# Attention of blocks two to six: four tiles' scores in one stretch of 32x64 tiles, one carried product for two heads

## The chip, the core and the metric

The kernel runs on one core of one Trainium2 chip. The metric is device time in microseconds (us) of one execution. Busy times and start times below come from one profiled execution of the kernel before. The engines are PE (TensorE, matmul), DVE (VectorE), ACT (ScalarE), POOL (GpSimd) and SP (SyncE, which only issues DMAs here); PEld is TensorE's weight load, which runs beside PE.

## What is computed

A gated linear attention over chunks of tokens feeds two feed-forward layers. Here batch is 4, H = 8 heads, S = 768 tokens, D = 32, N = 16; the kernel uses chunks of 64.

```python
for c in range(nc):                      # chunks, in order; a state [N, D] per head is carried
    L = np.exp(cum[:, :, :, None] - cum[:, :, None, :]) * causal
    M = np.einsum('bhin,bhjn->bhij', Cc, Bc) * L              # scores times decay
    y_intra = np.einsum('bhij,bhjd->bhid', M, xc)             # products
    y_inter = np.einsum('bhin,bhnd->bhid', Cc, state) * exp(cum)   # carried
    y[:, :, sl] = y_intra + y_inter
    state = decay_full * state + sum_j(Bc_j x_j decay_from_j)  # new state, then carry
x = y.transpose(0, 2, 1, 3).reshape(3072, 256)
h = x @ w_in;   x = np.maximum(0.01 * h, h) @ w_out           # first layer, 256 -> 2048 -> 256
h = x @ w_in2;  out = (h * np.cos(h)) @ w_out2                # second layer
```

## The kernel before

**Staging.** The tokens are cut into six blocks (b = 0 to 5 in the code, one to six here) of 4 batches x 128 tokens. A tile j is the 128 tokens of one batch in a block. Each block goes through attention, then a first-layer job, then a second-layer job; the jobs run in the order `JOBS = "000110101011"`. A job has 16 steps f, each a matmul group into `h` (lines 684 to 686: three products of high and low parts for each of two row halves) and one into `y` (lines 725 to 727). All are 128x512, in the first job and a half partly 128x256. Attention of block b+1 is put in between the steps of first-layer job b.

**Order.** All work is handed to a planner (class `Order`) with costs per engine, due times and slots of buffers. It fixes one order for each engine; on the chip each engine then takes its instructions in that order and waits on semaphores. PE order decides between which steps an attention stretch comes.

**Attention of a block.** For each tile: `scan` (line 466, DVE) makes the decays in `abc`; `bd` scales B in `tok`; `decay_c` (DVE or POOL) scales C in `head`. The two tiles of a pair then go through:

- `cb`, the scores (line 483): 8 matmuls of a tile, each with 64 rows of `head`, 64 weight columns and 128 columns of output, so that 64x64 pieces of the array work. `headp` has zeros where heads don't meet, and a row half r goes into columns 128r of a bank.
- `decay` (line 491, DVE): scores times decays, from PSUM into `abc`; one 128x512 operation for an even tile (in `att`, two banks), two of 128x256 for an odd one (in two `g` tiles of one bank).
- `products` (lines 504 and 508): 24 matmuls a tile, 64 rows by 32 weight columns by 64; lines 508 make the new state, 128x64 for each chunk s, where each 32 rows hold two heads.
- `carry` (line 542, DVE): old state times decay plus new state, read from PSUM.
- `carried` (line 517): 16 matmuls a tile, 32 rows by 32 columns by 64, each for one head and one chunk, so two heads share 32 state rows by having zeros in C.
- `x_hi` (line 529, ACT) and `x_lo` (line 533, DVE) take the pair's sum out of PSUM into `x1h` and `x1l`, the input of the next first-layer job.

In blocks two to six PE has five stretches of this: scores of pair one; products of pair one; carried of pair one together with scores of pair two; products of pair two; carried of pair two. Each matmul in fp32 stands as two passes in the trace (x16 for 8 matmuls).

## Time and profile before

| | us |
|---|---|
| median of 3 runs | 589.3 (589.26 to 589.36) |
| the profiled execution: span from first to last instruction | 586.7 |
| PE busy | 578.3 (99%) |
| PEld busy | 471.5 (80%) |
| ACT busy | 353.3 (60%) |
| DVE busy | 321.4 (55%) |
| POOL busy | 265.1 (45%) |

No device time is shown for the profiled execution itself, only its span; the median lies 2.6 us above that span. Busy PE is time with at least one matmul under way, ends modelled. The five attention stretches of blocks two to six lie at 53 to 75, 90 to 109, 141 to 160, 279 to 298 and 373 to 392 us.

### The profile page before, as it was taken

Reading aid. Unit: us, or ns where it says so; the run is one execution under the profiler, and the core shown is the slowest. Engines: PE = TensorE matmul, PEld = TensorE weight load, DVE = VectorE, ACT = ScalarE, POOL = GpSimd, SP = SyncE. Lnnn points to the kernel's source line nnn. Section 1 sums busy time; section 2 is a strip of 40 time slices with the busy share of each in tenths; the row PEclk is TensorE's granted clock in tenths of the full one; section 3 lists DMA queues with packets and bytes.
Section 4 is the critical chain, followed back from the end, with each engine's and each line's share of the span. In section 5 each row is a group of like instructions: output and inputs, shape, how many; then the busy total and the mean of one; then the engine's idle time right before and its main releaser. Section 6 shows DMA issues by size and latency. Waiting matters only on the chain.

```text
span 586.7 us, 11708 instructions
## 1 busy us (share of the span) xinstructions
PE 578.3 (99%) x4655; PEld 471.5 (80%) x4657; DVE 321.4 (55%) x610; ACT 353.3 (60%) x592; POOL 265.1 (45%) x224
## 2 busy tenths in 40 slices
PE   8899999999999999999999999999999999999996
PEld 4787887787788888888788888778888888888885
DVE  6999896845676656650464562121565002566664
ACT  4999767688856565554346554344755444655564
POOL 3221226188504455445525445443645444554442
PEclk9899999999999999999999999999999999999999
DMA  8994445543710001001330001000000100000101
GB/s 280 282 296 145 157 144 180 174 144 108 234 56 0 1 1 37 0 1 36 110 111 2 0 1 36 2 2 1 1 0 2 37 0 0 2 0 1 37 0 36
DMA packets 25798, 38.95 MB, mean 66 GB/s; under 512 B 2224, under 2 KB 8880, under 8 KB 25744
## 3 DMA queue, kind: packets, MB, share of 16 engines
q1 hardware_dynamic: 25744, 38.22, 20.6%
q8 instruction: 36, 0.59, 0.4%
q14 instruction: 18, 0.15, 0.1%
HBM read 34.96 MB, written 3.24 MB: 65 GB/s over the span
## 4 chain that ended last, share of the span: by engine, by line
PE 95%; DMA 2%; DVE 1%; SPq 0%; issue 0%; ACT 0%
PE y L725 15%; PE y L727 15%; PE y L726 15%; PE h L684 12%; PE h L685 11%; PE h L686 11%; PE g L686 4%; PE g L685 4%; PE g L684 4%; DMA tok<-tokp 1%; PE att L483 1%; PE att L517 1%; PE att L504 1%; PE g L483 1%; DMA head<-headp 1%; PE g L517 1%
## 5 line engine op out<-in xcount | busy, mean ns | idle before, releaser
L324 POOL TENSOR_TENSOR lo<-u,hi 128x512 fp32r<-128x512 f32 x156 | 204.8, 1315 | 235.5 <-DVE hi L318 90.7
L694 ACT ACTIVATE u<-h 128x512 f32<-128x512 f32 (+1 forms) x102 | 59.1, 581 | 83.5 <-PE h L686 77.5
L706 ACT ACTIVATE k<-k,half_pi 128x512 f32<-128x512 f32 (+1 forms) x97 | 69.8, 720 | 49.0 <-DVE k L701 48.2
L316 ACT ACTIVATE hi<-u 128x512 fp32r<-128x512 f32 (+1 forms) x124 | 75.7, 610 | 7.9 <-DVE u L710 2.4
L684 PE MATMUL h<-x1h,wi0h 128*128 128x512 f32 (+1 forms) x204 | 79.8, 391 | 0.0
L685 PE MATMUL h<-x1l,wi0h 128*128 128x512 f32 (+1 forms) x204 | 77.8, 382 | 0.1
L725 PE MATMUL y<-hi,wo0h 128*128 128x512 f32 (+1 forms) x204 | 77.8, 382 | 0.0
L686 PE MATMUL h<-x1h,wi0l 128*128 128x512 f32 (+1 forms) x204 | 77.4, 380 | 0.0
L727 PE MATMUL y<-lo,wo0h 128*128 128x512 f32 (+1 forms) x204 | 77.0, 377 | 0.0
L726 PE MATMUL y<-hi,wo0l 128*128 128x512 f32 (+1 forms) x204 | 76.9, 377 | 0.0
L725 PE MATMUL y<-hi,wo1h 128*128 128x512 f32 (+1 forms) x194 | 75.1, 387 | 0.0
L726 PE MATMUL y<-hi,wo1l 128*128 128x512 f32 (+1 forms) x194 | 75.1, 387 | 0.0
L727 PE MATMUL y<-lo,wo1h 128*128 128x512 f32 (+1 forms) x194 | 75.1, 387 | 0.0
L701 DVE SCALAR_TENSOR_TENSOR k<-k,h 128x512 f32<-128x512 int32 (+1 forms) x49 | 33.4, 682 | 73.3 <-ACT k L697 73.3
L710 DVE TENSOR_TENSOR u<-h,k 128x512 f32<-128x512 f32 (+1 forms) x49 | 33.6, 687 | 37.1 <-ACT k L706 35.8
L710 DVE TENSOR_TENSOR u<-g,k 128x512 f32<-128x512 f32 (+1 forms) x48 | 32.9, 686 | 32.8 <-ACT k L706 32.0
L697 ACT ACTIVATE k<-h 128x512 int32<-128x512 f32 (+1 forms) x49 | 29.0, 592 | 30.6 <-PE h L686 30.4
L684 PEld LDWEIGHTS h<-x1h,wi0h 128*128 128x128 f32 x204 | 39.0, 191 | 9.0 <-issue 1.2
L697 ACT ACTIVATE k<-g 128x512 int32<-128x512 f32 (+1 forms) x48 | 28.5, 593 | 27.2 <-PE g L686 27.1
L686 PEld LDWEIGHTS h<-x1h,wi0l 128*128 128x128 f32 x204 | 38.9, 191 | 7.2
L725 PEld LDWEIGHTS y<-hi,wo0h 128*128 128x128 f32 x204 | 38.3, 188 | 7.9 <-issue 0.2
L685 PEld LDWEIGHTS h<-x1l,wi0h 128*128 128x128 f32 x204 | 38.9, 191 | 6.7 <-DVE x1l L533 0.3
(131 smaller groups left out, 1060.2 us busy)
## 6 DMA issues: line engine op xcount, KB each, us to landing
head<-headp SPq DMA_DIRECT2D x24, 256.0 KB, 4.7
tok<-tokp SPq DMA_DIRECT2D x24, 256.0 KB, 4.3
raw<-w_out SPq DMA_DIRECT2D x12, 512.0 KB, 4.0
raw<-w_in SPq DMA_DIRECT2D x11, 512.0 KB, 4.4
abc<-a_clip SPq DMA_DIRECT2D x40, 128.0 KB, 3.6
out_t<-u SPq DMA_DIRECT2D x10, 256.0 KB, 2.7
x2h<-w_in SPq DMA_DIRECT2D x4, 512.0 KB, 5.3
x2l<-w_out SPq DMA_DIRECT2D x4, 512.0 KB, 6.3
```

What stands on the lines that cost most here:

```text
L316: A.activation(out, in_, AF.Copy, scale=scale, bias=bias)
L324: G.tensor_tensor(out=out, in0=a, in1=b, op=op)
L684: PE.matmul(o, lhsT=wh, rhs=xh, start=(c == 0), stop=False)
L685: PE.matmul(o, lhsT=wh, rhs=xl, start=False, stop=False)
L686: PE.matmul(o, lhsT=wl, rhs=xh, start=False, stop=(c == 1))
L694: A.activation(make(u, "u", [128, n], F32)[:, 0:m], tiles[h][:, 0:m], AF.Prelu, alpha=0.01)
L697: A.activation(make(k, "k", [128, n], I32)[:, 0:m], tiles[h][:, 0:m], AF.Copy, scale=INV2PI, bias=0.25)
L706: A.activation(t, t, AF.Sin, bias=half_pi)
L710: V.tensor_tensor(out=t[:, 0:m], in0=tiles[h][:, 0:m], in1=tiles[k].bitcast(F32)[:, 0:m], op=ALU.mult)
L725: PE.matmul(o, lhsT=wh, rhs=gh, start=(f == q.start == 0), stop=False, **skip)
L726: PE.matmul(o, lhsT=wl, rhs=gh, start=False, stop=False, **skip)
L727: PE.matmul(o, lhsT=wh, rhs=gl, start=False, stop=(f == KF - 1), **skip)
```

## The change

Blocks two to six are written anew in a class `Block`; block one keeps the old form.

- Scores: `headp` now holds B, C and C masked to even and odd heads. `all_cb` does 8 matmuls a tile with 32 rows, 64 weight columns and 128 columns of output; row group r goes to bank r (`att` has banks 0 and 1, the two `g` tiles are 2 and 3). All four tiles stand in one PE stretch, with tile j in columns 128j of each bank.
- `decay` takes a tile out of three PSUM tiles: one 128x256 and two 128x128 operations.
- `products`: the same 24 matmuls a tile, with y in columns 64j and the new states in columns 256 to 383 of the banks. Heads are in natural order, so `w_in` is no longer permuted. A planner entry of 2.5 (`APART`) keeps the two pairs apart.
- `mask` (new, DVE): new states of all four tiles times a constant `own` (zero where the state belongs to the other head of the two) go from PSUM to `tok`; `carry` reads them there. Block one's last states are multiplied by `own` once.
- `all_carried`: 8 matmuls a tile instead of 16, 32 rows by 64 weight columns by 64, each for two heads, all four tiles in one stretch.
- `decay_c` scales one copy of C (128x128) instead of two.
- `x_hi` and `x_lo` run per chunk s over all four tiles: one 128x512 operation and two of 128x256 in place of two of 128x256 and four of 128x128.
- `const_own` (new, POOL, at the start): a memset and eight small selects.

```diff
@@ headp @@
-        headp[:, :, h, :, h // 2 % 2] = Bc[:, :, h].transpose(0, 1, 3, 2)
+        headp[0, :, h, :, h // 2 % 2] = Bc[0, :, h].transpose(0, 2, 1)
+        headp[1:, :, h, :, 0] = Bc[1:, :, h].transpose(0, 1, 3, 2)
+        headp[1:, :, h, :, 1] = Cc[1:, :, h].transpose(0, 1, 3, 2)
         headp[:, :, h, :, 2 + h % 2] = Cc[:, :, h].transpose(0, 1, 3, 2)
@@ class TokenTile @@
+        def all_cb(self, first):
+            k = tiles[self.head]
+            for c in range(0, T, Q):
+                for r in range(4):
+                    rows = slice(32 * r, 32 * r + 32)
+                    PE.matmul(self.block.bank(r)[c:c + Q, 128 * self.j:128 * self.j + 128].rearrange("p (q i) -> p q i", q=2),
+                              lhsT=k[rows, c:c + Q], rhs=k[rows, 2 * T:4 * T].rearrange("p (q i) -> p q i", q=2)[:, :, c:c + Q],
+                              start=first, stop=True, skip_group_check=True)
...
+        def all_carried(self):
+            for s in range(2):
+                for r in range(4):
+                    o, rows = 64 * (r % 2), slice(32 * r, 32 * r + 32)
+                    PE.matmul(self.block.bank(2 * s + r // 2)[o:o + 64, Q * self.j:Q * self.j + Q], lhsT=tiles[self.st[s]][rows, :],
+                              rhs=tiles[self.head][rows, T + Q * s:T + Q * s + Q], start=False, stop=True, skip_group_check=True)
@@ class Block @@
+        def mask(self, s):
+            o = tiles[self.tt[s].tok][:, 0:256].rearrange("p (n j c) -> p n j c", n=2, j=2)
+            for i, n, t in self.parts():
+                if i // 2 == s:
+                    V.tensor_tensor(out=o[:, i % 2:i % 2 + n], in0=t[:, :, 256:384].rearrange("p n (j c) -> p n j c", j=2),
+                                    in1=own.rearrange("p (n j c) -> p n j c", n=1, j=1).to_broadcast([128, n, 2, 2 * D]), op=ALU.mult)
@@ attention(), blocks two to six @@
+            on_pe(1.25, tt, [k.fresh, *(lambda x=x: x.all_cb(x.j == 0) for x in tt)], ...
+            for i in (0, 2):
+                on_pe(1.35, tt[i:i + 2], [x.products for x in tt[i:i + 2]], ...
+            for s in range(1 if b == NBLK - 1 else 2):
+                od.add(None, {"V": 0.36 + 0.1 * s}, lambda e, s=s: k.mask(s), ...
+            for x in tt:
+                x.carries()
+            on_pe(1.2, tt, [x.all_carried for x in tt], ...
```

How the order moves, at two places of block three.

PE, from the end of pair one's products to the next big step (`att` and `g` are PSUM tiles, `st` the states, `head` the scaled C and B). Before, carried of pair one and scores of pair two in one stretch:

```order
L725 MATMUL y_1252<-hi_1428,wo0h_71 128x512
L726 MATMUL y_1252<-hi_1428,wo0l_72 128x512
L727 MATMUL y_1252<-lo_1456,wo0h_71 128x512
L517 MATMUL att_81<-head_1039,st0_1037 32x64 x4
L517 MATMUL g_1438<-head_1039,st0_1037 32x64 x4
L517 MATMUL att_81<-head_1039,st0_1536 32x64 x4
L517 MATMUL g_1439<-head_1039,st0_1536 32x64 x4
```

Now, the one carried stretch of the block, which begins the same way for each of the four tiles:

```order
L822 MATMUL y_1259<-hi_1570,wo0h_71 128x512
L823 MATMUL y_1259<-hi_1570,wo0l_72 128x512
L824 MATMUL y_1259<-lo_1579,wo0h_71 128x512
L606 MATMUL att_82<-head_1148,st0_1150 64x64 x4
L606 MATMUL g_1425<-head_1148,st0_1669 64x64 x2
L606 MATMUL g_1426<-head_1148,st0_1669 64x64 x2
L606 MATMUL att_82<-head_1164,st1_1153 64x64 x4
L606 MATMUL g_1425<-head_1164,st1_1671 64x64 x2
```

Sixteen matmuls of a tile became eight of twice the width, and twelve big matmuls now lie between the second products and this stretch.

DVE between the same products and carried. Before, only carries:

```order
L326 TENSOR_TENSOR lo_1526<-u_1469,hi_1475 128x512
L374 SCALAR_TENSOR_TENSOR k_1450<-k_1450,raw_1392 128x512
L542 SCALAR_TENSOR_TENSOR st0_1536<-st0_1037,tok_1055,att_81 128x64
L542 SCALAR_TENSOR_TENSOR st1_1542<-st1_1041,tok_1064,g_1438 128x64
L542 SCALAR_TENSOR_TENSOR st0_1622<-st0_1536,tok_1055,att_81 128x64
```

Now, the masks and four carries that read what the masks wrote:

```order
L337 TENSOR_TENSOR wi1l_70<-k_1465,wi1h_69 128x2x256
L385 SCALAR_TENSOR_TENSOR k_1559<-k_1559,raw_1461 128x512
L471 TENSOR_TENSOR tok_1174<-att_82,own_78 128x256
L471 TENSOR_TENSOR tok_1193<-g_1425,own_78 128x128
L471 TENSOR_TENSOR tok_1193<-g_1426,own_78 128x128
L632 SCALAR_TENSOR_TENSOR st0_1669<-st0_1150,tok_1174 128x64
L632 SCALAR_TENSOR_TENSOR st1_1671<-st1_1153,tok_1193,tok_1174 128x64
L632 SCALAR_TENSOR_TENSOR st2_1676<-st2_1158,tok_1208,tok_1174 128x64
L632 SCALAR_TENSOR_TENSOR st3_1684<-st3_1166,tok_1221,tok_1174 128x64
```

Seven DVE operations now stand between a products stretch and the carried stretch, in a row with nothing else among them.

## Rows read from the trace of the kernel before

**Rows 1.** Page, part 1: busy us, share of the span, instructions.
```profile
PE 578.3 (99%) x4655; PEld 471.5 (80%) x4657; DVE 321.4 (55%) x610; ACT 353.3 (60%) x592; POOL 265.1 (45%) x224
```
**Rows 2.** Page, part 4: the chain that ended last, by engine.
```profile
PE 95%; DMA 2%; DVE 1%; SPq 0%; issue 0%; ACT 0%
```
**Rows 3.** Windows: busy us of PE, PEld, DVE, ACT, POOL; granted clock; DMA.
```profile
20.00:22.00 2.00, 2.00 (x23) 1.80 (x15) 2.00 (x5) 2.00 (x6) 1.79 (x2) 0.50 0.98 289
...
35.00:53.00 18.00, 18.00 (x81) 14.70 (x79) 17.54 (x29) 17.69 (x28) 2.61 (x3) 1.00 0.81 241
53.00:77.00 24.00, 24.00 (x476) 19.76 (x475) 21.05 (x52) 18.37 (x35) 8.51 (x8) 1.00 0.39 132
```
**Rows 4.** PE timeline, block three, first scores: start us, duration us, instruction.
```profile
87.21 0.39 PE L684 MATMUL h<-x1h,wi0h 128*128 128x512 f32 x1
...
89.70 0.39 PE L727 MATMUL y<-lo,wo0h 128*128 128x512 f32 x1
90.02 0.67 PE L483 MATMUL att<-head 64*64 64x128 f32 x16
...
91.05 0.50 PE L684 MATMUL h<-x1h,wi0h 128*128 128x512 f32 x1
91.39 0.40 PE L685 MATMUL h<-x1l,wi0h 128*128 128x512 f32 x1
```
**Rows 5.** PE timeline, block three, products of pair one.
```profile
93.72 0.39 PE L727 MATMUL y<-lo,wo0h 128*128 128x512 f32 x1
94.04 0.34 PE L504 MATMUL att<-abc,tok 64*32 64x64 f32 x16
...
95.55 0.39 PE L685 MATMUL h<-x1l,wi0h 128*128 128x512 f32 x1
```
**Rows 6.** PE timeline, block three, carried of pair one with scores of pair two.
```profile
97.84 0.39 PE L727 MATMUL y<-lo,wo0h 128*128 128x512 f32 x1
98.16 0.26 PE L517 MATMUL att<-head,st 32*32 32x64 f32 x4
...
98.94 0.67 PE L483 MATMUL att<-head 64*64 64x128 f32 x16
...
100.31 0.39 PE L685 MATMUL h<-x1l,wi0h 128*128 128x512 f32 x1
```
**Rows 7.** PE timeline, block six, carried of pair two.
```profile
390.19 0.40 PE L727 MATMUL y<-lo,wo0h 128*128 128x512 f32 x1
...
391.64 0.40 PE L685 MATMUL h<-x1l,wi0h 128*128 128x512 f32 x1
```
**Rows 8.** PE timeline, block three, carried of pair two: a wait inside the stretch.
```profile
108.20 0.24 PE L517 MATMUL att<-head,st 32*32 32x64 f32 x1 [0.38 <-issue]
```
**Rows 9.** DVE timeline, block one: sizes that the change uses, from PSUM.
```profile
10.33 0.73 DVE L491 TENSOR_TENSOR abc<-g,abc 128x256 f32<-128x256 f32 x2
...
14.21 0.48 DVE L533 TENSOR_TENSOR x1l<-g,x1h 128x128 fp32r<-128x128 f32 x2
...
16.29 0.67 DVE L491 TENSOR_TENSOR abc<-att,abc 128x512 f32<-128x512 f32 x1
...
20.58 0.27 DVE L542 SCALAR_TENSOR_TENSOR st<-st,tok,att 128x64 f32<-128x64 f32 x1
20.77 0.27 DVE L542 SCALAR_TENSOR_TENSOR st<-st,tok,g 128x64 f32<-128x64 f32 x1
```
**Rows 10.** DVE timeline, block three: one operation on SBUF data, alone and held up.
```profile
92.91 0.68 DVE L374 SCALAR_TENSOR_TENSOR k<-k,raw 128x512 uint32<-128x512 uint32 x1
...
94.74 1.78 DVE L374 SCALAR_TENSOR_TENSOR k<-k,raw 128x512 uint32<-128x512 uint32 x1
```
**Rows 11.** DVE timeline, block one: a wait ahead of the second pair's scans.
```profile
15.04 0.20 DVE L288 TENSOR_SCALAR tok<-tok 128x64 f32<-128x64 f32 x1 [0.36 <-DMA tok<-tokp]
```
**Rows 12.** PE timeline, block one: products of the second pair.
```profile
17.01 0.35 PE L504 MATMUL att<-abc,tok 64*32 64x64 f32 x16 [0.65 <-DVE abc L491]
...
18.47 0.35 PE L504 MATMUL att<-abc,tok 64*32 64x64 f32 x16 [0.73 <-DVE st L539]
```

More of the change, by code (lines that the diff above doesn't have):

```diff
@@ L45 @@
 PAIR = 0.3
+APART = 2.5
 TAIL = 2
-OUT_HEADS = [[2 * p for p in range(4)], [2 * ((p + 2) % 4) + 1 for p in range(4)]]
 PSUM_TAGS = {"h": 2, "g": 2, "y": 2}
@@ L450, in decay_c @@
         def decay_c(self, e):
+            if not self.first:
+                o = tiles[self.head][:, T:2 * T]
+                times(e, o, o, tiles[self.tok][:, 384:512])
+                return
             c = Q * self.s0
@@ L535, in carry @@
         def carry(self, e, s):
-            new, st = bank(self.t, s)[:, 384:448], self.st
+            st = self.st
+            new = self.new_state(s) if self.first else tiles[self.block.tt[s].tok][:, 64 * self.j:64 * self.j + 64]
             o = make(st[s + 1], f"st{self.j}", [128, 2 * D], F32)
@@ L597, in on_pe @@
             od.add(None, {"P": cost}, go, reads=reads, writes=writes, make=make, slack=min(x.slack for x in group))
-        def scores(group, cost, steps=(), reads=(), writes=()):
-            new = [(n, "g") for x in group if x.j == 1 for n in att_names(x.t)]
-            on_pe(cost, group, [*steps, *(x.cb for x in group)],
-                  [*reads, *(x.head + k for x in group for k in ("/b", "/c")), *([] if first else [f"run{b - 1}"]),
-                   *keys([x for x in group if x.j > 1 or (b and x.j == 0)], "/y")],
-                  [*writes, *keys(group, "/cb"), *(n + "/y" for n, _ in new)], new)
```

152 lines of the change are left out of this document (106 added, 46 removed).

## Prediction, on record before the changed kernel ran

> **What bounds the kernel now.** First the busy line [rows 1]: PE is busy 578.3 of 586.7 us and every other engine at most 60%. Then the chain that ended last [rows 2]: 95% of it is PE. So time comes off only where PE's own work gets shorter or PE waits less, and each us that PE saves outside the start and the tail is a us of the whole. Then the PE timeline of one block's attention [rows 4 to 7], read from start to start, since matmuls overlap. Eleven steps from 87.21 to 89.70 give 0.226 us for one 128x512 matmul [rows 4]. An attention stretch costs the time from the last big matmul ahead of it to the second one behind it, less two ordinary steps (0.45 us); the second one, because the first one behind it starts late as well.
>
> **The change on PE, stretch by stretch.** Before, in block three:
> - first scores: 91.39 - 89.70 - 0.45 = 1.24 us for 32 passes [rows 4];
> - products of a pair: 95.55 - 93.72 - 0.45 = 1.38 for 96 passes [rows 5]; the second pair has the same 96 passes and is taken at the same price;
> - carried with scores: 100.31 - 97.84 - 0.45 = 2.02 for 64 and 32 passes [rows 6];
> - last carried, read in block six, where no wait stands in it: 391.64 - 390.19 - 0.45 = 1.00 for 64 passes [rows 7].
>
> Together 1.24 + 1.38 + 2.02 + 1.38 + 1.00 = 7.02 us a block, five times. Scores and carried apart cost 1.24 + 1.00 = 2.24, in one stretch 2.02; so a stretch of its own costs 0.22 (the emptying ahead of it, the late start behind it), and the passes alone cost 1.02 / 32 = 32 ns (scores), 1.16 / 96 = 12.1 ns (products), 0.78 / 64 = 12.2 ns (carried).
>
> After, a block has 64 score passes in one stretch, 2 x 96 of products and 64 of carried, 320 instead of 384.
> - Scores. A pass has the same 128 columns, but 32 rows instead of 64, so eight pieces of the array can work beside each other where four do now. With 32 ns on four pieces, eight give 16 ns: 64 x 16 + 0.22 = 1.24. Bounds: 12.1 ns, the quickest pace that any small pass has here [rows 5], gives 1.00; 32 ns, no gain from more pieces, gives 2.27.
> - Carried. 64 passes of 64 columns, on four of the eight pieces (row group r with column half r % 2). The scores before are also four pieces, with 128 columns; half the columns gives 16 ns and 1.24 us. Bounds again 1.00 and 2.27. I take 16 and not 12.2, since the 12.2 was reached with 32-column weights on sixteen pieces.
> - Products keep forms and number: 2 x 1.38.
>
> Sum 1.24 + 2.76 + 1.24 = 5.24, so 1.78 us less a block, 8.9 over five. At both low bounds 7.02 - 4.76 = 2.26 a block, 11.3; at both high bounds 7.02 - 7.30, a loss of 0.28 a block, 1.4.
>
> The wait of 0.38 us inside one carried stretch [rows 8] is counted neither way: nothing names its cause, and it can come back elsewhere.
>
> **A rule on banks.** In the carried stretch before, four heads in the four row groups write four partition groups of one bank (line 517 and `y_cols`), and its passes still come at 12.2 ns each. The Trainium skill, TensorEngine Tiling (Array Packing), section Gotcha 1: PSUM Pressure, says that different row tiles cannot access one PSUM bank at the same time; the new carried puts two row groups into each bank. By that rule the trace before would show turns, and at 12.2 ns a pass of 64 columns it shows none that could be told, so I give it little.
>
> **The change on DVE.** A decay costs now 0.67 (even tile) or 0.73 (odd) [rows 9]; after, one 128x256 (half of 0.73) and two 128x128 (0.48 as a pair) for each: 0.85. Four tiles: 3.4 against 2.8, +0.6. Masks: 0.85 a block more. Carries keep their 0.20 pitch (20.58 to 20.77 [rows 9]) if reading SBUF instead of PSUM costs the same. `x_lo` goes from 2 x (0.37 + 0.48) = 1.7 to 0.67 + 0.73 = 1.4. So DVE gets about 1.2 us more a block. In the fullest stretch with attention, block two, it is busy 21.05 of 24 us [rows 3], 2.95 free. ACT loses work: fewer operations in `x_hi`. `decay_c` halves on POOL and DVE. These hide beside PE as long as they are not late.
>
> **Where PE can wait anew.** Behind the second products stand, on DVE, three mask operations and four carries, then all of carried: 0.85 + 4 x 0.20 = 1.65. A handover from DVE to PE took 0.05 (16.29 + 0.67 to 17.01) [rows 9, 12]; with one at each end I take 1.8. PE has twelve big matmuls to do meanwhile, 12 x 0.226 = 2.7 us: 0.9 to spare. But one DVE operation on SBUF data took 1.78 instead of 0.68 [rows 10], 1.1 more; such a hold in the chain makes PE wait 0.2. Queued behind the waiting carried matmuls on PE are the next first-layer steps, so all wait. Decays have eighteen big matmuls (4.1 us) for the two tiles that the first products need (1.7). I put 0.8 for new waits in the five blocks together (0 to 3).
>
> Loads: the scores need four `head` tiles at once instead of two, and SP issues them together with `tok` and `abc`; the four slots come free when the carried stretch of the block before ends, and from there to the next scores lie 15 us or more (the attention of block two ends at 75 us, the scores of three begin at 90.02 [rows 4]), so the queue moves but nobody waits.
>
> Block one and the start: `const_own` is among POOL's first instructions, before any load has come, and costs nothing as long as POOL has no data to wait on; the multiplications by `own` and a reordered DVE queue are another matter. DVE now does one 128x512 operation (0.68 [rows 10]) ahead of the scan that the second pair of block one waits for, after the wait for a load [rows 11], and PE stands waiting for that pair (0.65 and 0.73 [rows 12]). Part is caught up behind it; I put 0.3 us (0 to 0.7). The clock granted is 0.50, the 1.2 GHz level, at 20 to 22 us [rows 3], after those pauses, and can rise somewhat later or sooner: 1 us either way.
>
> **Sum.** 8.9 - 0.8 - 0.3 = 7.8 us. The span would be 586.7 - 7.8 = 578.9 us; the median of the runs stood 2.6 above the span, which the change doesn't touch: 589.3 - 7.8 = 581.5 us.
>
> **Rivals.**
> - Block two's share is eaten: DVE and ACT prepare weights beside it (busy 17.54 and 17.69 of 18 us ahead of it [rows 3]) and its 1.2 us more make the first layer's `lo` or the block's inputs late. For it: hardly a gap is left there. Against it: PE is busy 18.00 of 18 and 24.00 of 24 us there [rows 3], and 2.95 us were free on DVE. Block two gains nothing: 581.5 + 1.8 = 583.3.
> - Banks take turns in carried: two of its four pieces at a time, 32 ns a pass: 2.27 instead of 1.24, +1.03 x 5 = 5.2: 586.7. For it: two row groups to a bank. Against it: the 12.2 ns before.
> - The change doesn't do what it says: 32x64 pieces run no denser than 64x64 ones, weights of 64 columns being the limit, 32 ns in both stretches: 589.3 + 1.4 + 0.3 = 591.0; with only part of it, no change. Against it: with 32-column weights, eight or sixteen pieces did come to 12 ns.
> - Slower by a new wait: the seven DVE operations read SBUF that POOL also uses, and several are held. Three holds of 1.1 in each block make the chain 1.8 + 3.3 = 5.1 against 2.7, so PE waits 2.4 us, 12 in all: 589.3 + 12 - 8.9 + 0.3 = 592.7. It decides from 2.7 + 1.8 = 4.5 us on, where the wait eats the block's 1.78. For it: rows 10. Against it: nothing else is queued among the seven, masks read PSUM, and carries took 0.27 each before.
>
> **How the numbers follow.** Forecast 0.67; block two 0.10; banks 0.08; no denser 0.08; held DVE 0.07. The forecast's own range is 579 to 584 (waits 0 to 3, clock 1, pace 14 to 18 ns: 2 x 64 x 2 ns x 5 = 1.3). The full range of 578.0 to 587.0 takes in block two and banks and the lower pace bound but for its last us, and leaves out some 0.17. Within 0.2% (1.2 us), about what a measurement of this kernel can't tell from none, is 588.1 to 590.5. Faster 0.67 + 0.10 + 0.08 = 0.85; the rest splits into 0.06 same (partly denser, or fewer holds) and 0.09 slower.
>
> **What would show it.** In the profile after: score stretches of about 1.0 us from first to last start, at 16 ns a pass; carried the same; products unchanged at 1.38; no idle on PE ahead of line 606 (carried) and 585 (products); DVE's masks done some 0.8 us after the products. PE busy near 570. Scores over 2 us say the pieces don't overlap; carried alone over 2 us says banks; idle time ahead of line 606 with DVE operations over 0.5 us says holds. The prediction is wrong if a stretch that I took as unchanged grows, or if the first 20 us lose more than 1 us.

## The result, and the profile after

| | before | after |
|---|---|---|
| median of 4 runs, us | 589.28 (588.75 to 589.36) | 582.78 (581.60 to 585.54) |
| ratio | | 0.9894 [0.9866, 0.9922] |
| span of the profiled execution, us | 586.7 | 581.9 (its own time: 583.61) |

The kernel became 6.5 us faster, 1.3 us less than forecast. Its four times lie 3.9 us apart and those of before 0.6, but eleven more runs of before, taken beside `again`, lie between 589.12 and 592.54, so a wider spread of the changed kernel is not shown.

Spans and medians don't differ by the same amount, and the record says why. Where both stand on record, the time of an execution of before is 1.7 to 1.9 us above its span, in after 1.7 to 1.8. So the profiled execution of before took some 588.5 us (an estimate, 586.7 + 1.8), 0.8 less than the median of its kernel, and that of after took 583.61, 0.8 more than its median. The 2.6 us "above that span" in the section on the time before are the 1.8 and this 0.8, no fixed distance.

Page of after: the span, the busy line (answers to [rows 1]), the DMA queue that brings instructions, and the chain (answers to [rows 2]).

```profile
span 581.9 us, 11085 instructions
PE 571.2 (98%) x4338; PEld 465.7 (80%) x4338; DVE 331.7 (57%) x631; ACT 349.7 (60%) x573; POOL 275.8 (47%) x248
q8 instruction: 34, 0.56, 0.4%
PE 96%; DVE 2%; issue 1%; ACT 0%; DVEq 0%
```

PE is busy 7.1 us less, but the span fell by only 4.8: 2.3 us more of it are idle. PE's waits in after say where:

```profile
PE att L599 <- issue: 1.1, 1, 1.1
PE g L541 <- issue: 1.1, 1, 1.1
...
PE g L606 <- issue: 0.3, 1, 0.3
...
PE y L824 <- DVE lo L337: 0.3, 1, 0.3
PE h L781 <- ACT u L791: 0.2, 1, 0.2
```

Lines 541 and 599 are block one, whose attention code the change left alone; 606 is the new carried stretch. The first two rows, "issue", wait for nothing that the profile names.

Windows of after, as [rows 3]: busy us of PE, PEld, DVE, ACT, POOL; granted clock; DMA.

```profile
35.00:53.00 18.00, 18.00 (x140) 14.70 (x138) 17.56 (x30) 17.97 (x30) 2.31 (x3) 1.00 0.66 211
53.00:77.00 24.00, 23.50 (x360) 18.80 (x349) 22.94 (x54) 22.04 (x38) 12.70 (x11) 1.00 0.62 199
```

PE was never idle from 53 to 77 us; now it is for 0.5, with DVE busy 1.9 and ACT 3.7 us longer there.

The stretches themselves. PE timeline of after, block three, first scores (answers to [rows 4]):

```profile
91.32 0.39 PE L824 MATMUL y<-lo,wo0h 128*128 128x512 f32 x1
91.63 0.33 PE L551 MATMUL att<-head 32*64 32x128 f32 x2
...
92.77 0.50 PE L781 MATMUL h<-x1h,wi0h 128*128 128x512 f32 x1
93.11 0.40 PE L782 MATMUL h<-x1l,wi0h 128*128 128x512 f32 x1
```

93.11 - 91.32 - 0.45 = 1.34 for all four tiles' scores. The carried stretch of block five, where nothing waits (answers to [rows 7]):

```profile
291.60 0.39 PE L824 MATMUL y<-lo,wo0h 128*128 128x512 f32 x1
...
292.78 0.29 PE L606 MATMUL g<-head,st 32*64 32x64 f32 x8
293.00 0.50 PE L822 MATMUL y<-hi,wo0h 128*128 128x512 f32 x1
293.34 0.40 PE L823 MATMUL y<-hi,wo0l 128*128 128x512 f32 x1
```

293.34 - 291.60 - 0.45 = 1.29. In block three the same stretch took 1.66 (answers to [rows 8]); its row for the last eight passes lasts 0.66 instead of 0.29, since a wait lies within it:

```profile
105.61 0.39 PE L824 MATMUL y<-lo,wo0h 128*128 128x512 f32 x1
...
106.79 0.66 PE L606 MATMUL g<-head,st 32*64 32x64 f32 x8
107.38 0.50 PE L822 MATMUL y<-hi,wo0h 128*128 128x512 f32 x1
107.72 0.39 PE L823 MATMUL y<-hi,wo0l 128*128 128x512 f32 x1
```

In block four it took 1.91, with 0.35 <-issue at 156.65. Products (as [rows 5]), which the change left alone, took 1.31 where they took 1.38 before, and 1.38 once in block two.

**Where the time went.** Both kernels have 2388 big matmuls (the steps of the two layers), all but 90 of them in the same order, so the start of one can be compared with that of the same number; at the numbers of the table both have done the same steps. The table gives the start in the kernel before, and how much later (+) or earlier (-) the same one starts in after and in three kernels of the experiments (again is after itself, once more).

| big matmul | before, us | after | again | old_cost | join_first |
|---|---|---|---|---|---|
| 73, end of the start | 30.50 | +2.94 | +1.40 | +0.42 | +0.91 |
| 301, behind block two | 82.39 | +1.61 | +0.38 | +0.19 | +0.85 |
| 401, behind three | 112.21 | -0.39 | -1.13 | -1.42 | -0.98 |
| 601, behind four | 164.76 | -1.54 | -2.98 | -3.27 | -2.79 |
| 1181, behind five | 303.58 | -3.42 | -4.87 | -5.17 | -4.66 |
| 1561, behind six | 396.88 | -5.18 | -6.67 | -6.97 | -6.42 |
| 2388, the last | 581.91 | -5.18 | -6.66 | -6.96 | -6.42 |

So in after the start lost 2.94 us, blocks two to six gave back 1.33, 2.00, 1.15, 1.88 and 1.76 (8.12 together), and the tail lost 0.3. Between the blocks the difference stays the same. There is only one trace of before, and its execution took some 0.8 us less than the median, so part of the 2.94 may lie in that one execution.

### The profile page after: what moved, and what is told of

It is laid out like the page before. It is cut to its first block, busy times and chain, and to the rows that moved or that the text cites. A ratio compares the mean times of both kernels' runs of the same rounds, so it can differ in the third digit from the quotient of the medians.

```text
span 581.9 us, 11085 instructions
## 1 busy us (share of the span) xinstructions
PE 571.2 (98%) x4338; PEld 465.7 (80%) x4338; DVE 331.7 (57%) x631; ACT 349.7 (60%) x573; POOL 275.8 (47%) x248
## 4 chain that ended last, share of the span: by engine, by line
PE 96%; DVE 2%; issue 1%; ACT 0%; DVEq 0%
PE y L822 15%; PE y L824 15%; PE y L823 15%; PE h L781 12%; PE h L782 11%; PE h L783 11%; PE g L783 4%; PE g L781 4%; PE g L782 4%; PE h L286 1%; PE att L585 1%; PE att L551 1%; PE g L585 0%; PE att L606 0%; DVE st L632 0%
## 5 line engine op out<-in xcount | busy, mean ns | idle before, releaser
L335 POOL TENSOR_TENSOR lo<-u,hi 128x512 fp32r<-128x512 f32 (+1 forms) x163 | 212.0, 1303 | 241.3 <-DVE hi L329 91.9
L781 PE MATMUL h<-x1h,wi0h 128*128 128x512 f32 (+1 forms) x204 | 78.4, 384 | 0.3 <-ACT u L791 0.2
L824 PEld LDWEIGHTS y<-lo,wo0h 128*128 128x128 f32 x204 | 38.7, 190 | 8.0 <-DVE lo L337 0.7
```

Of the source, the lines that this page charges most:

```text
L335: G.tensor_tensor(out=out, in0=a, in1=b, op=op)
L781: PE.matmul(o, lhsT=wh, rhs=xh, start=(c == 0), stop=False)
L824: PE.matmul(o, lhsT=wh, rhs=gl, start=False, stop=(f == KF - 1), **skip)
```

## Experiments: the start and block two

Block one does not keep quite its old form: the change also lowered the planner's cost of `decay_c` for all blocks, block one among them (that line does not stand in the diff shown ahead of the prediction). With the old number there, the first 60 or so instructions of DVE and ACT stand in the order of before. Theory: this order is the start's loss.

**again** is the changed kernel, unchanged.

> The changed kernel once more, unchanged. Its four runs of the result lay at 581.6, 581.95, 583.61 and 585.54 us, those of the kernel before within 0.6 us. Theory F (PE's instructions come late): the profiled run lost 2.9 us in the first 25 us, with two waits of 1.05 and 1.11 us inside block one that nothing but the fetching of PE's instructions explains; how long such a wait is hangs on the loads that are under way, so it differs from run to run. Then the times again spread over 2 to 4 us, block three's and block four's carried stretches again cost 1.6 to 1.9 us instead of 1.30, and the two waits stand at the same passes of block one (the last of the second scores, pass 23 of the second carried), shorter or longer. Rival N (one disturbed run): the waits are gone or stand elsewhere, times within 0.5 us around 581.6.

Measured: 583.97 us, median of 6 (582.11 to 586.41), ratio 0.9901 [0.9875, 0.9926]. Of the waits that were expected to come again, only that of block three did (2.19 for its carried stretch); block four took 1.30. Its profiled execution has no issue wait in block one, and its start loses 1.40 instead of 2.94. So 1.5 us of after's start are not the order. Five runs described below have after's own order up to block two, which gives seven executions of one start: without issue waits of 0.2 us or more in block one it lost 1.30 (masks), 1.33 (loads5) and 1.40 (again), and with 1.6 to 2.6 us of them 2.94 (after), 3.04 (orders), 3.81 (forms) and 4.94 (raws5).

**old_cost** gives block one its old planner cost:

```diff
-            od.add(None, {"Gx": 0.42, "Vx": 0.2}, self.decay_c, reads=[tok + "/p", head + "/c"],
+            od.add(None, {"Gx": 0.75 / (1 + self.s0), "Vx": 0.34 / (1 + self.s0)} if self.first else {"Gx": 0.42, "Vx": 0.2}, self.decay_c, reads=[tok + "/p", head + "/c"],
```

> One number: the planner's cost of the decay of c in block one is what it was before the change (0.75 and 0.375 for POOL, 0.34 and 0.17 for DVE; the change gave it 0.42 and 0.2 in every block). With it DVE's and ACT's order in the first blocks is that of the kernel before. Theory S (the order of block one costs the start): the first big matmul stands at 15.4 us as before and not at 17.7, the first one behind block one's carried products at 20.4 and not 22.8, no wait for instructions over 0.3 us ahead of 25 us; the time falls by 2 to 3 us, to 579.5 to 581 us, and the spread between runs falls below 1 us. Rival M (the multiplications by own on POOL, which stay, cost the start): the same start as the changed kernel, 582 to 584 us. Rival N (chance): the same as the changed kernel, whose times lie at 581.6 to 585.5.

Measured: 582.59, median of 4 (581.93 to 583.42), 0.9878 [0.9852, 0.9903], so the expected 579.5 to 581 did not come. Its times lie 2.1 to 2.2 us above their spans instead of 1.7, for a reason that no run shows, so 0.4 us of its earlier end in the table are not seen in its time. The start lost only 0.42, although one issue wait of 1.1 us is among it. But block two gained 0.23 instead of 1.0 to 1.3. DVE rows of old_cost, and the PE row that follows from them:

```profile
51.03 0.41 DVE L559 TENSOR_TENSOR abc<-att,abc 128x256 f32<-128x256 f32 x1
...
53.94 1.56 DVE L385 SCALAR_TENSOR_TENSOR k<-k,raw 128x512 uint32<-128x512 uint32 x2
...
56.09 0.50 PE L781 MATMUL h<-x1h,wi0h 128*128 128x512 f32 x1 [1.05 <-ACT wi0h L327]
```

Here DVE does the four tiles' decays (51.03 to 53.94) ahead of joining the weights in line 385; ACT makes `wi0h` from those, and PE waits 1.05 us for it.

**join_first** is old_cost with the decays of block two due 2 us later, so that the joins come first:

```diff
-                   reads=[*([self.att + "/cb"] if self.first else self.block.keys("/cb")), ab], writes=[ab], slack=slack)
+                   reads=[*([self.att + "/cb"] if self.first else self.block.keys("/cb")), ab], writes=[ab], slack=slack - 2.0 * (self.b == 1))
```

> The old planner's cost of block one's decay (as in old_cost) and, in block two alone, two us less slack for the four decays, which puts one of the two joins of weights (line 385) ahead of them on DVE instead of behind. In old_cost the four decays ran from 51.03 to 53.94 us with both joins behind them, and PE waited 1.05 us for the wi0h that ACT makes of them. Theory Q (block two's share is eaten by DVE's order): that wait is gone, block two gains 1.0 to 1.3 us against the kernel before instead of 0.2, and the time is 1 us below old_cost's 582.6: about 581.5, below the changed kernel's 582.8 to 584.0. Rival L (DVE is simply full there, and what goes ahead makes something else late): another wait of about 1 us takes its place, decays or lo, and the time stays at 582 to 583.

Measured: 582.40, median of 5 (581.50 to 583.83), 0.9876 [0.9848, 0.9905]. The wait for `wi0h` is gone, and this one stands in its place (with one of 0.51 for `x1l` at 72.45):

```profile
54.53 0.32 PE L585 MATMUL att<-abc,tok 64*32 64x64 f32 x8 [0.45 <-DVE abc L559]
```

Block two gained 0.06. What follows: the order of block one does cost the start something, 0.4 to 1.0 us: 1.30 to 1.40 with the new order and no issue waits, 0.42 in old_cost and 0.91 in join_first, which have the same old order there. The granted clock is not the cause: from 18 to 28 us its mean is 0.83 in before, after, again and masks and 1.00 in old_cost, join_first and loads5, and loads5 lost 1.33 all the same. Window of again, then of loads5:

```profile
18.00:28.00 10.00, 8.68 (x171) 7.73 (x172) 8.22 (x19) 9.62 (x22) 5.43 (x7) 0.83 0.92 276
```

```profile
18.00:28.00 10.00, 7.86 (x173) 7.06 (x174) 7.94 (x18) 10.00 (x23) 5.47 (x7) 1.00 0.96 268
```

Why 0.42 to 0.91 stay lost with the old order, no run shows. Getting the rest back doesn't shorten the whole by as much. Behind block two, again stands at +0.38, old_cost at +0.19, join_first at +0.85. Up to there DVE and ACT are full ([rows 3], and the window of after), and whichever work goes first, the other comes late. The ratios of old_cost and join_first lie within the intervals of the changed kernel's, so neither is shown to be faster than it.

## Experiments: the issue waits

Where a wait is "issue" and a packet of the DMA queue q8 (kind "instruction") ends shortly ahead, TensorE may be waiting for its own instructions. After has 4338 matmuls and as many weight loads, 8,676, and q8 has 34 packets: some 255 a packet, 16 KB each (0.56 MB / 34). In the trace of after such a packet ends at 15.99, 21.25 and 155.15; the waits end at 17.41, 22.58 and 156.65, 1.3 to 1.5 us later each time. The wait in before [rows 8] ends at 108.20, 1.5 us behind a packet that ended at 106.70. A few short issue waits, such as one of 0.25 us in before at 12.35, have no such packet ahead; they are not meant here.

**shift16** puts 16 more small matmuls, and so 32 instructions, into the warm-up ahead of everything (some of 64 columns in place of long ones). If the wait comes at a fixed count of instructions, it must come 16 passes earlier in each stretch.

```diff
-        PE.matmul(tiles["warm"][:, 0:WARM_N], lhsT=tiles["zero"][:, 0:128], rhs=tiles["zero"][:, 0:WARM_N], start=True, stop=True)
+        n, times_i = (64, {1: 5, 2: 4, 3: 4, 4: 4, 5: 4}[i]) if i in {1: 5, 2: 4, 3: 4, 4: 4, 5: 4} else (WARM_N, 1)
+        for _ in range(times_i):
+            PE.matmul(tiles["warm"][:, 0:n], lhsT=tiles["zero"][:, 0:128], rhs=tiles["zero"][:, 0:n], start=True, stop=True)
```

> Five of the warm-up matmuls of PE's first us are split into 21 short ones, so 16 matmuls and 16 weight loads (32 instructions) more stand ahead of everything; nothing else differs. Theory F: PE's waits inside the carried stretches of block three (0.37 us too much) and four (0.62) come at a fixed count of PE's instructions (256 apart, the 16 KB of one packet of its instruction queue), so they now come 16 passes earlier in the same stretches: about pass 42 instead of 58 in block three and pass 40 instead of 56 in block four. Less big matmuls lie between the asking and the need then, so they grow, to some 0.8 and 1.3 us: stretches of 2.1 and 2.6 us. Block five's comes near as well, without loads under way, and stays at 1.30. Rival D (the stretch waits for something of its own, a state or a semaphore): the waits stay at passes 58 and 56, stretches of 1.66 and 1.91.

Measured: 583.30, median of 4 (581.98 to 587.51), 0.9897 [0.9863, 0.9931]. In again the wait of block three stands ahead of pass 59 of the 64, as in after; here ahead of pass 43. PE timelines of again and of shift16 (8 passes a row up to the wait):

```profile
105.52 0.28 PE L606 MATMUL g<-head,st 32*64 32x64 f32 x2
106.37 0.34 PE L606 MATMUL g<-head,st 32*64 32x64 f32 x6 [0.57 <-issue]
```

```profile
105.80 0.28 PE L608 MATMUL g<-head,st 32*64 32x64 f32 x2
106.82 0.28 PE L608 MATMUL g<-head,st 32*64 32x64 f32 x3 [0.74 <-issue]
```

7 x 8 + 2 = 58 passes lie ahead of the first, 5 x 8 + 2 = 42 ahead of the second. That block four would wait longer (2.6 us for its stretch) didn't come: 1.30, no wait.

**shift33** does the same with 33 more matmuls.

> The same with ten of the warm-up matmuls split into 43 short ones: 66 instructions more ahead of everything. Theory F: the places of the waits move by 33 passes to the front, to about pass 25 of block three's carried stretch and pass 23 of block four's, where nearly 2.5 us more of big matmuls lie between the asking and the need, so both waits vanish: all five carried stretches at 1.30 us, 1.0 us less in blocks three and four together. In block one the waits move out of the second scores and the second carried products to the warm-up ahead of the scores and to the second products; how much is lost there is open. Rival D: the waits stay, 1.66 and 1.91.

Measured: 584.08, median of 4 (581.03 to 584.38), 0.9886 [0.9860, 0.9913]. The waits of blocks three and four are gone (1.29 and 1.30), but the start lost 4.67, with TensorE at half pace after the thinned warm-up. The first window row is of shift33, the second of after:

```profile
8.00:22.00 14.00, 13.33 (x195) 7.39 (x195) 10.35 (x28) 7.80 (x17) 3.40 (x5) 0.51 0.82 277
```

```profile
8.00:22.00 14.00, 10.95 (x316) 6.59 (x316) 13.06 (x36) 10.64 (x24) 5.90 (x8) 1.00 0.94 323
```

The granted clock was 0.51, so the 1.2 GHz level, and PE did 195 matmuls where after did 316.

**less8** leaves out 8 of the warm-up matmuls, which moves the count the other way; **old_cost_less8** does that and takes old_cost's line.

```diff
-        PE.matmul(tiles["warm"][:, 0:WARM_N], lhsT=tiles["zero"][:, 0:128], rhs=tiles["zero"][:, 0:WARM_N], start=True, stop=True)
+        if i not in range(1, 9):
+            PE.matmul(tiles["warm"][:, 0:WARM_N], lhsT=tiles["zero"][:, 0:128], rhs=tiles["zero"][:, 0:WARM_N], start=True, stop=True)
```

> The changed kernel without eight of the eleven warm-up matmuls of the first 5 us (16 instructions fewer ahead of everything). Theory F: the fixed count falls 8 passes later: pass 67 of block three's carried stretch and 66 of block four's, of 64 passes, so both waits move behind the stretch among big matmuls that take 0.11 us an instruction and are hidden or nearly so: stretches of 1.30 to 1.5 instead of 1.66 to 2.2 (three) and 1.30 to 1.9 (four). In block one the count falls behind the second scores and on the last pass of the second carried: a loss at the start of 0.5 to 2 us. TensorE does less at first; if the granted clock falls for it in the first 10 us, the start costs up to 1 us more. Rival D (the waits belong to the stretches): they stay.

> The old planner's cost of block one's decay together with eight warm-up matmuls fewer. Theory F: the wait of 1.12 us at pass 26 of block one's second carried products falls to pass 34 of 32, behind it, and so does block three's (pass 64 to 72): 1.5 us less in the profile than the kernel with the old cost alone, so 580 to 581 us in the median instead of 582.6. What stays is its wait of 1.05 us in block two for a weight that ACT makes. Rival: the lost warm-up costs clock in the first 10 us and takes it back: 582 to 583.

Measured: 586.65, median of 4 (584.81 to 587.38), and 585.66, median of 4 (585.20 to 586.36). Neither became faster, as old_cost_less8 should have: no issue wait over 0.5 us was left in block one, and the carried stretches of blocks three and four took 1.30 and 1.56 in less8, 1.29 and 1.30 in old_cost_less8, but the start lost 4.75 and 4.33, at half pace again. Rows of less8's PE timeline, first sixteen passes of the size that [rows 4] shows with 0.67, then the steps behind block three's carried stretch:

```profile
18.96 1.13 PE L542 MATMUL att<-head 64*64 64x128 f32 x16
...
109.52 0.40 PE L824 MATMUL y<-hi,wo0l 128*128 128x512 f32 x1
112.02 0.40 PE L825 MATMUL y<-lo,wo0h 128*128 128x512 f32 x1 [2.10 <-issue]
```

Block three's wait did not vanish. It stands ahead of the third big matmul behind the 64 passes, so ahead of matmul 67 where it was ahead of 59: exactly the eight places later that were expected. It was not hidden there but cost 2.10 us, 1.3 us behind a packet that ended at 110.69, and block three gave less8 only 0.10 us.

**raws5** asks whether loads under way make a packet late. In block five, which has no wait, it issues two loads of 512 KB into spare places about 5 us ahead of the carried stretch:

```diff
+                    if b == 4:
+                        for q in range(2):
+                            def spare(e, q=q):
+                                t = make(f"spare{q}", "raw", [128, 2, 256, 2], U32)
+                                A.dma_start(out=t.rearrange("p k f w -> p k (f w)"),
+                                            in_=w_in.rearrange("(k p) f -> p k f", p=128)[:, :, 512 * q:512 * q + 512])
+                            od.add(None, {"A": 0.1}, spare, reads=[f"apart{b}"], writes=[f"spare{q}"], make=[(f"spare{q}", "raw")], slack=tt[0].slack)
...
```

A further line of this edit, not shown, has the planner put the carried stretch behind the issue of these loads.

> Block five of this kernel issues two loads of 512 KB into spare places about 5 us ahead of its carried stretch, so that the DMA engines are busy over the point at which TensorE's next packet of instructions is brought. Theory F (a packet that comes late because loads are under way makes the issue waits of blocks three and four): the packet that in the changed kernel starts at about 289 us, with the DMA engines quiet, starts 1 us or more later, and the carried stretch of block five, or a stretch up to 3 us behind it, shows an issue wait of 0.3 to 1 us; block five costs that much more. Theory N (the point of the packet is set by how far TensorE has come, and loads don't move it): it starts within 0.5 us of that point, no issue wait in block five, carried stretch 1.30. One look: 582 to 585 us either way.

Measured, one run: 586.80; its start lost 4.94 with an issue wait of 2.20 us, so the time says little and block five is read by itself. A window and the PE timeline of raws5, which stands 1.7 us behind after ahead of block five, then the window of after:

```profile
290.00:292.00 2.00, 2.00 (x71) 1.69 (x67) 0.30 (x1) 0.30 (x1) 1.29 (x1) 1.00 1.09 337
...
294.51 0.29 PE L606 MATMUL att<-head,st 32*64 32x64 f32 x7
295.84 0.21 PE L606 MATMUL att<-head,st 32*64 32x64 f32 x1 [1.04 <-issue]
```

```profile
288.00:290.00 2.00, 2.00 (x101) 1.72 (x87) 1.43 (x6) 0.57 (x1) 1.28 (x1) 1.00 0.12 38
```

With the DMA engines full (share 1.09 against 0.12), the packet that begins 6.11 us after the one ahead of it in after (282.91 to 289.02) began 8.68 us after (284.45 to 293.13). It ended at 294.37, and the new wait ended at 295.84, 1.5 us later. In the five other executions with as many matmuls up to there (again, masks, loads5, forms, orders) that packet began 5.97 to 6.40 us after the one ahead of it. The carried stretch took 2.70 instead of 1.29. So the wait can be made where there was none.

**loads5** was a first form of this test, with four copies of 512 KB from and to the chip's memory, issued by ACT.

```diff
+                    if b == 4:
+                        for i_ in range(4):
+                            od.add(None, {"A": 0.1}, lambda e, i_=i_: A.dma_start(out=spare[i_], in_=headp[2 * i_:2 * i_ + 2]),
+                                   reads=[f"apart{b}"], writes=[f"spare{i_}"], slack=tt[0].slack)
...
```

> The changed kernel with four copies of 512 KB from HBM to HBM more, which nothing reads, issued by ACT once, between the first products and the carried products of block five; every other instruction stands where it did. In block five the fixed count of PE's instructions falls on about pass 54 of the carried stretch, but no loads are under way there (DMA busy 0.12 from 288 to 290 us in the changed kernel) and the stretch cost 1.30 us in all seven kernels that had it unchanged; in block three, with loads under way (0.78), the count at pass 59 cost 0.2 to 2.2 us. Theory F (the packet of PE's instructions queues behind the other transfers): block five's carried stretch gets a wait for instructions at pass 54 or so, of 0.3 to 2 us, ending some 1.4 us after the packet; it costs 1.6 to 3.3 us instead of 1.30. Rival G (block three's place differs by something else, the engines' own work or the order of passes): block five stays at 1.30 with DMA busy around it.

Measured, one run: 590.68. Inconclusive for block five: ACT was held 13 us, PE waited 3.7 us for it, the DMA engines were only 0.36 to 0.39 busy from 288 to 294 us, the packet began 6.22 us behind the one ahead of it (6.11 in after), and the stretch stayed at 1.29. Block three, which the edit leaves alone, had an issue wait of 2.06 us in this execution, again ahead of pass 59.

What follows: the issue waits behind a packet are TensorE out of instructions. They come at a fixed count in the program (16 more matmuls ahead: 16 places earlier; 8 fewer: 8 places later), and only in some executions or places, by how late the packet is; loads make it late (one run). What sets the point at which a packet is asked for, the runs don't show.

## Experiments: the price of a pass, and DVE's chain

**forms** changes one form in each block, and so part of its output: in block three each row group writes a bank of its own, in block four a carried pass has 32 columns and leaves out the other half, in block five the carried passes use all eight pieces, and in block six the scores are 128 passes of 64 columns.

```diff
+                    n = 1 if self.b == 5 else 2
+                    for q in range(0, 2, n):
...
+                    if self.b == 2:
+                        bk, c = r, 256 * s + Q * self.j
+                    if self.b == 3:
+                        n = Q // 2
+                    if self.b == 4:
+                        o = 64 * ((r + s) % 2)
```

> Another form in each block, so the results of the scan are others from block three on and the time is not to be compared; read are the stretches. Block two: carried and scores unchanged (1.30 and 1.34 us). Block three: in carried every row group writes a bank of its own instead of two to a bank. Block four: carried passes of 32 columns instead of 64 (half of the carried part is left out). Block five: the column half that a row group uses is swapped for the second half of the tile, so all eight pieces of the array are used instead of four. Block six: scores as 128 passes of 64 columns instead of 64 passes of 128. Theory W (a 32x64 pass costs its own 13 to 15 ns whatever its columns: 64 columns of weights to be loaded): blocks three, four and five stay at 1.30, block six's scores rise to 0.4 + 128 x 13.8 ns = 2.2 us. Theory C (the time of the columns on the pieces decides): block four falls to about 1.0 (half the columns), block five to about 1.0 (twice the pieces), block three stays, block six's scores stay at 1.34. Rival B (two row groups to a bank take turns): block three falls to about 1.0, block five stays.

Measured, one run: 587.89. Carried in block four 1.27, in five 1.12, against 1.29 or 1.30; scores in six 2.13 against 1.34, so 0.79 / 64 = 12.3 ns for each pass more. Block three took 4.17, with a wait ahead of pass 59 again:

```profile
106.99 0.22 PE L614 MATMUL att<-head,st 32*64 32x64 f32 x2
...
107.64 0.28 PE L614 MATMUL att<-head,st 32*64 32x64 f32 x2
110.07 0.26 PE L614 MATMUL att<-head,st 32*64 32x64 f32 x1 [2.16 <-issue]
...
111.07 0.63 PE L831 MATMUL y<-hi,wo0l 128*128 128x512 f32 x1
```

The stretch's cost is spoiled by the wait, but its pace is not: 44 passes in 107.64 - 106.99 = 0.65 us, 14.8 ns each, with a bank for each row group. In after, two row groups to a bank, 48 passes took 106.79 - 106.09 = 0.70, 14.6 ns. All four row groups in one bank couldn't be laid out without two of them meeting in the same partitions, so it wasn't tried.

**orders** changes only the order of the passes.

```diff
+            if self.b in (1, 5):
+                o = [(c, r) for r in range(4) for c in range(0, T, Q)]
+            if self.b == 3:
+                o = [(Q * (r % 2) ^ c, r) for c in range(0, T, Q) for r in range(4)]
...
+            if self.b in (1, 5):
+                order = [(s, r) for s in range(2) for r in (0, 2, 1, 3)]
+            if self.b == 4:
+                order = [(s, r) for r in range(4) for s in range(2)]
```

> The same passes in another order, same result. Scores: blocks two and six take both column halves of a row group before the next row group; block four takes the column halves in turns, so that eight pieces are started within four passes of each other; three and five unchanged. Carried: blocks two and six take row groups 0, 2, 1, 3; block five takes both halves of a tile for each row group; three and four unchanged. Theory W (a pass costs its own 12 to 14 ns, whatever its piece): all scores 1.34, all carried 1.30 apart from waits for instructions. Rival C (passes that follow each other on the same row group or column half wait for each other): scores of blocks two and six go to 1.6 us or more, block five's carried to 1.5 or more.

Measured, one run: 583.35. All scores 1.34, carried 1.29 to 1.30, but 1.44 in block five, where both passes of a row group follow each other, and 1.80 in block three by an issue wait, ahead of pass 59. So a 32x64 pass has its own price of 12 to 15 ns, the same within some 1 ns for 32, 64 and 128 columns (64 passes in 1.27, 1.30 and 1.34 us), in nearly any order; in the carried stretch all eight pieces instead of four save 0.18 us in 64 passes. What sets this price, the runs don't show.

**masks** does a block's mask operations several times over, to use up DVE's cover: twice in block three, three times in five, seven times in six.

```diff
-                od.add(None, {"V": 0.36 + 0.1 * s}, lambda e, s=s: k.mask(s), reads=["own", *k.keys("/s")], writes=[tt[s].tok + "/x"], slack=tt[0].slack)
+                od.add(None, {"V": 0.36 + 0.1 * s}, lambda e, s=s: [k.mask(s) for _ in range({1: 1, 2: 2, 3: 1, 4: 3, 5: 7}[b])], reads=["own", *k.keys("/s")], writes=[tt[s].tok + "/x"], slack=tt[0].slack)
```

> DVE does the masks of a block several times over (same result): twice in block three, once in four, three times in five, seven times in six. Each further time costs 0.79 us on DVE (0.34 in block six, where only one half is masked), read at 103.01 to 103.75 of the changed kernel's trace, and it lies between the second products and the carried ones. My term: DVE's chain took 1.62 us there of 2.9 us of cover (twelve big matmuls), so 1.3 us are to spare. Then block three (chain 2.4) still waits for nothing, block five (3.2) waits some 0.3 us ahead of its carried stretch, block six (1.6 + 2.0 = 3.7) some 0.7; the stretches themselves stay at 1.30. Rival R (DVE is no part of it: the carried stretch waits on loads or on the fetching of instructions): no wait ahead of carried in blocks five and six either.

Measured, one run: 582.75. No wait on DVE in three, none in five (a wait of 0.3 was expected there), 0.9 us in block six. DVE and PE timelines of masks, block six:

```profile
379.15 3.17 DVE L471 TENSOR_TENSOR tok<-att,own 128x256 f32<-128x256 f32 x7 [7.14 <-PE att L589]
382.36 1.89 DVE L632 SCALAR_TENSOR_TENSOR st<-st,tok 128x64 f32<-128x64 f32 x4
...
382.38 0.34 PE L606 MATMUL att<-head,st 32*64 32x64 f32 x8 [0.22 <-DVE tok L471]
384.31 0.34 PE L606 MATMUL g<-head,st 32*64 32x64 f32 x8 [0.68 <-DVE st L632]
```

Carried begins with its first tile as soon as that tile's carry is done; the other carries finish beside it. In block five the last carry ended at 290.03, 0.38 us behind the first carried pass (in after at 290.61, 1.30 ahead of it), and nothing waited. So the cover is larger than the prediction's.

## Why the prediction was right, and where it was not

The forecast of 581.5 (its own range 579 to 584) was right in sign and within its range. The blocks gave what the sum said, the start lost far more than it said, and the 582.78 lies in the range because the range had room for that.

- **The stretches: right.** Scores 1.34, products 2 x 1.31 and carried 1.30 are 5.26 a block; the sum said 5.24. It was made of wrong parts, though. Scores and carried cost 0.10 and 0.06 more than the 1.24 put for each, and the products, taken as unchanged, 0.07 less a pair, which is luck. A pass costs 12 to 15 ns and a stretch some 0.4 to 0.5 of its own, instead of 16 and 0.22; at the 64 passes of a stretch both come to nearly the same. That half the columns would halve 32 ns fell: at 32x64 the columns don't matter (forms). Scores on eight pieces and carried on four have about the same pace.
- **Banks: rightly given little.** Carried with two row groups to a bank ran at 14.6 ns a pass, with one each at 14.8. The Trainium skill, TensorEngine Tiling (Array Packing), section Gotcha 1: PSUM Pressure, says that different row tiles cannot access one PSUM bank at the same time. These two paces show no turns.
- **No denser pieces: fell.** 64 score passes took 1.34, not 2.27.
- **DVE's chain behind the second products: right, with more to spare than 0.9.** The one hold over 0.5 us among the four carries ahead of a carried stretch, in block four, cost PE nothing, and in masks the chain of block five ended 1.7 us later without a wait. DVE timeline of after, block four (the carries stand held, 1.95 instead of 0.88, until 154.99; carried began at 155.22 with no wait):

```profile
153.04 1.95 DVE L632 SCALAR_TENSOR_TENSOR st<-st,tok 128x64 f32<-128x64 f32 x4
```

- **The wait of 0.38 counted neither way: it did come back elsewhere**, as instruction waits that cost 0.4 and 0.6 us in blocks three and four. It had itself made block three's last stretch 1.61 instead of 1.00 before (106.73 to 108.79, less 0.45), which is why that block gave 2.00. The five blocks gave 8.12, where 8.9 less 0.8 for waits had been put; the size is right, the waits are of another kind.
- **The start: the step that failed.** I put 0.3 us (0 to 0.7) for block one and its reordered DVE queue. It was 1.30 to 1.40 in the three executions without instruction waits, and 2.94 (after) to 4.94 in the four with them. The operation that the term rested on is there: `k<-k,x2h` stands ahead of the scan. But x1l was late ahead of it already, at 15.12 instead of 14.21 [rows 9], since DVE had two operations more to do (`head<-head,tok`, the re-costed `decay_c`, and a cast of `wi0h`) and a wait for PE. DVE timeline of after:

```profile
12.63 0.28 DVE L337 TENSOR_TENSOR head<-head,tok 128x128 f32<-128x128 f32 x1
...
13.60 0.28 DVE L632 SCALAR_TENSOR_TENSOR st<-st,tok,g 128x64 f32<-128x64 f32 x1 [0.25 <-PE g L599]
...
14.00 0.27 DVE L329 CAST wi0h<-k 128x256 fp32r<-128x256 f32 x1
...
15.12 0.48 DVE L622 TENSOR_TENSOR x1l<-g,x1h 128x128 fp32r<-128x128 f32 x2
...
15.61 0.68 DVE L385 SCALAR_TENSOR_TENSOR k<-k,x2h 128x512 uint32<-128x512 uint32 x1
16.21 1.22 DVE L524 TENSOR_TENSOR_SCAN abc<-y,ident 128x512 f32<-128x512 f32 x1
```

  The scan of before, with nothing but the short operation of [rows 11] between x1l and it:

```profile
15.15 1.22 DVE L466 TENSOR_TENSOR_SCAN abc<-y,ident 128x512 f32<-128x512 f32 x1
```

  So the scan came 1.06 us late, and little of that was caught up. In old_cost x1l is at 14.92 and the scan at 15.51, and the start lost 0.42. On PE two waits that no term had stand in the same place of after:

```profile
17.41 0.32 PE L541 MATMUL g<-head 64*64 64x128 f32 x1 [1.05 <-issue]
...
22.58 0.24 PE L599 MATMUL att<-head,st 32*32 32x64 f32 x1 [1.11 <-issue]
```

- **The clock, 1 us either way: no difference.** It fell and rose again in after too, some 4 us later: 0.50 from 24 to 26 us, and 0.83 on the mean from 18 to 28 us in both.
- **Block two eaten (583.3): half right.** Block two gained 1.33, not nothing. But start and block two together stand at -0.03 (masks) and +0.38 (again) without instruction waits, at +1.61 in after, where 0.3 - 1.8 = -1.5 had been put, and the two kernels that mended the start lost the gain of block two. That is the rival's mechanism, DVE and ACT full ahead of and beside block two, one place earlier than it was looked for. By the traces the truth lies nearer to this rival than to the forecast; the median of 582.78 is 0.5 us from it and 1.3 from the forecast.
- **The 2.6 us between span and time: no term of the change, and not a constant** (see the result). It stands on both sides of the forecast and cancels there. Against the profiled execution of before alone, the changed kernel gained 4.8 us in span in after and 6.3 in again, where 7.8 had been put.

The condition that I gave for being wrong, "the first 20 us lose more than 1 us", did come true, and that the median still lies within 579 to 584 owes something to luck: that of again, 583.97, lies at the upper edge. Open remain why packets are late in some executions of block one, what costs the 0.42 to 0.91 that stay lost with the old order, and whether any order of the first 80 us would free DVE and ACT enough to keep both gains.

## What to carry to other kernels

Count 32x64 fp32 passes, not their columns (32 to 128 cost the same here): in block six the scores took 1.34 us in 64 passes of 128 columns and, in forms, 2.13 in 128 passes of 64. To the passes come some 0.4 to 0.5 us for each stretch that stands alone between big matmuls. Where DVE and ACT are full, as here up to 80 us, a change that only re-costs one planner entry there can move more than the edit that it came with, and mending one wait makes the next. Compare the start of same-numbered big steps in two traces before explaining any difference: it showed at once that 8 us came from the blocks and 3 had gone at the start.

## What the runs showed of the hardware that I had not expected

- Stretches of small passes can run TensorE out of instructions: a packet of 16 KB for some 255 instructions, waits of 0.2 to 2.2 us that end 1.2 to 1.6 us behind a packet's end, at a count that moves by exactly as many matmuls as are put ahead or left out.
- Such a wait can cost more than itself. Behind the 2.16 us of forms the granted clock was 0.50 from 110 to 113 us, and seven 128x512 steps took 3.0 us (110.48 to 113.50) where 1.7 are usual; behind the 2.06 of loads5 it was 0.50 from 110 to 112. Behind the 2.10 of less8 and the 1.04 of raws5 it stayed at 1.00. What tells them apart, the runs don't show.
- TensorE ran at half pace until about 22 us when its warm-up was thinned: in shift33 with a granted clock of 0.51, in less8 with the same durations (1.13 instead of 0.67 us) while that column reads 1.00. The trace of less8 has no record of the clock ahead of 21.66 us, so there the durations tell, and the column does not.
- A 32x64 pass costs the same with 32, 64 or 128 columns: 64 of them took 1.27, 1.30 and 1.34 us.
